# Decode attention and gated MLP on one core: a query weight shared by two key units, projections with one weight load per two banks, small inputs as long packets

## The chip, the core, the metric

One Trainium2 chip, of which the kernel uses one core of eight. The metric is the device time of one execution in microseconds (us). All times below are medians of several executions.

The engines are named as the profile does: PE is the matmul engine (PEld its weight loads), DVE the vector engine, ACT the scalar engine, SP the engine that issues the large DMAs.

## The reference, cut to what matters

One token (`S = 1`, `D = 1024`) goes through two branches, mixed by a scalar gate.

```python
g = sigmoid((x * gate_w).sum(-1))                     # gate_w [1024]
# branch A: 32 query heads, 4 key/value heads, 65536 cached keys of 128 elements
q = x @ wq                                            # wq [1024, 4096]
scores = einsum(q, repeat(k_cache)) * 128 ** -0.5     # k_cache [4, 65536, 128]
o = einsum(softmax(scores), repeat(v_cache))          # v_cache [4, 65536, 128]
a = o @ wo                                            # wo [4096, 1024]
# branch B
z = gelu(x @ w_in)                                    # w_in [1024, 3584]
z2 = layernorm(z[1792:])
b = (z[:1792] * (w_sp * z2 + b_sp)) @ w_out           # w_out [1792, 1024]; w_sp and b_sp are one value each
out = g * a + (1 - g) * b
```

Everything is bf16. The two caches are 67.1 MB each, all inputs together 162.0 MB. Each byte is used once.

## The kernel before

All engines are driven by a small recorder: `P(engine, function, r=reads, w=writes)` appends an operation. Each engine executes its operations in program order, and a semaphore wait is put in where a read or a write conflicts with an operation of another engine.

All large inputs pass through a ring of five SBUF slots of up to 4 MB, in one fixed order. A slot is loaded again as soon as its content has been used.

```python
small(vw(xT, 0, [[4, 2], [1, 4]]), A_x[0, 0].rearrange("(i p k) -> p i k", i=2, k=4), "xT")      # 8-byte pieces
small(vw(gw, 0, [[4, 2], [1, 4]]), gate_w.rearrange("(i p k) -> p i k", i=2, k=4), "gw")
small(wb[:, 0:1], bass.AP(tensor=B_w_sp.tensor, ..., ap=[[0, 128], [1, 1]]), "wsp")              # 128 x 2 bytes
small(wb[:, 1:2], bass.AP(tensor=B_b_sp.tensor, ..., ap=[[0, 128], [1, 1]]), "bsp")
# ... gate from xT and gw, then the wq matmuls; both need xT; program order puts the gate first
```

A key unit is 8192 keys. DVE transposes it in four pieces; each piece needs four matmuls whose weights are the padded query:

```python
def k_piece(n, j):                      # unit n, piece j
    P("DVE", lambda e: e.transpose(ktb(i).bitcast(F32), sl[:, 2048 * j:2048 * (j + 1)].bitcast(F32)), ...)
    def f(e):
        for fe in range(4):
            ins = e.matmul(pf(sb), qpad[g % 2][:, o:o + 128], vw(ktb(i), ...), ...)   # 128 columns, 512 wide
```

The output projection packs four matmuls into four column groups of the array, so that they run side by side (in the trace of the kernel before the first four start within 0.01 us, at 369.18 us):

```python
WO = [(0, 0, 8), (1, 0, 8), (2, 0, 8), (3, 0, 4), (3, 4, 6), (3, 6, 8)]     # chunk, first and last column
for i, c0, c1 in WO:
    for c in range(c0, c1):
        for q in range(4):
            e.matmul(pf(FB)[32 * q:32 * q + 1, 0:QW], ovec[:, 8 * i + c:...], sl[:, o:o + QW],   # QW = 256
                     tile_position=(0, 32 * q), ...)
P("DVE", lambda e: e.tensor_tensor(orow[0:97, :], pf(FB)[0:97, 0:QW], brow[0:97, :], ALU.add), ...)
```

The projection `w_out` of branch B ("wout" below) is packed in the same way into another bank, and is copied to `brow`.

## Time and profile before

| | before |
|---|---|
| time, median of its first 3 runs | 387.75 us (387.69 to 387.80) |
| span of the profiled run | 385.9 us |
| large DMA queue | 162.01 MB, 98.1% of 16 engines |
| PE, DVE busy | 59%, 55% |
| last V pair in use from | 363.2 us |

The last row is the time at which PE starts on the last load of values (one load brings a pair of value units); behind it only `wo` is still to come, in four chunks of 2 MB.

First some lines of the profile's page: the span and the busy times, the rate in 40 equal slices, the DMA queues (packets, MB, share), and two groups of instructions (busy us, mean ns of one, then the idle time before them and what ended it).

```profile
span 385.9 us, 3595 instructions
PE 227.0 (59%) x1542; PEld 84.7 (22%) x1542; DVE 210.5 (55%) x326; ACT 30.6 (8%) x71; POOL 2.1 (1%) x9
...
GB/s 326 435 435 442 374 442 426 429 436 433 435 408 419 435 435 430 428 435 427 431 431 435 433 435 431 435 423 429 435 431 426 428 432 435 430 431 428 419 419 190
...
q1 hardware_dynamic: 6200, 162.01, 98.1%
...
q10 hardware_dynamic: 832, 0.00, 0.1%
...
L457 PE MATMUL pb<-arena 128*128 128x512 bf16 x512 | 154.4, 442 | 78.5 <-DVE arena L449 76.2
L449 DVE STREAM_TRANSPOSE arena<-arena 128x1024 f32<-128x1024 f32 x128 | 151.3, 1216 | 56.7 <-DMA arena<-in_A_k_cache_dram 50.5
```

No compute engine is near full, and the DMA engines are: the stream is the limit. PE waits for DVE, and DVE for keys. At 431 GB/s the 162.0 MB take 376 us. Two slices stand out: the fifth (374) and the last.

The windows view shows this in three stretches. Its columns: start and end, length, busy time (and instructions) of PE, PEld, DVE, ACT and POOL, granted PE clock, DMA share, GB/s.

```profile
42.00:47.00 5.00, 4.87 (x48) 1.63 (x52) 0.08 (x1) 0.00 (x0) 0.00 (x0) 1.00 0.80 315
100.00:120.00 20.00, 15.95 (x115) 5.88 (x113) 19.16 (x30) 2.27 (x3) 0.00 (x0) 1.00 0.99 419
148.00:340.00 192.00, 121.80 (x684) 38.12 (x680) 121.59 (x175) 19.33 (x48) 0.00 (x0) 0.81 1.00 431
```

The steady rate is 431. The stretch of 42 to 47 us is slow at 315. I call it the hole. (The clock column of the first line says nothing: this trace has no clock record before 47.7 us, and the wq matmuls of that stretch step at 427 ns, the step of half clock.)

The chain that ended last, followed back from the end (start, length, what):

```profile
1.24 38.87 DMA arena<-in_gate_w_dram
...
42.13 6.39 PE pb L404 x64
...
146.17 1.04 PE pb L457 x4
...
369.25 1.83 PE pb L635 x28
371.08 0.02 issue
371.10 11.62 DMA arena<-in_A_wo_dram
382.72 0.04 issue
382.76 0.62 PE pb L635 x7
383.38 0.02 issue
383.41 0.42 DVE arena L641
```

A 2 KB input, `gate_w`, takes 38.9 us, and the first wq matmul (L404) comes only after it. At the end the kernel waits for the last bytes of `wo`; only 1.1 us of compute follows their landing (0.62 of packed matmuls, 0.42 of the final add).

### The profile page before, as it was taken

What the parts mean: (1) busy time and instruction counts of PE and PEld (TensorE: products, weight loads), DVE (VectorE), ACT (ScalarE), POOL (GpSimd) and SP (SyncE); (2) the same over time, 40 slices, a digit from 0 to 9 for tenths busy, and PEclk for the clock granted to TensorE, in tenths of its full rate; (3) what the DMA queues carried; (4) which work ended last, traced back from release to release, by engine and by line L of the source; (5) the groups of instructions that cost most, each with busy time, mean ns of one, the idle gap of its engine ahead of it and who ended that gap; (6) DMA issues with size and microseconds to landing.
All of it is one profiled execution on the core that took longest, in us unless ns stands there. A gap on an engine that the chain in (4) does not pass through costs nothing.

```text
span 385.9 us, 3595 instructions
## 1 busy us (share of the span) xinstructions
PE 227.0 (59%) x1542; PEld 84.7 (22%) x1542; DVE 210.5 (55%) x326; ACT 30.6 (8%) x71; POOL 2.1 (1%) x9
## 2 busy tenths in 40 slices
PE   0000668983886888472688383827883929543354
PEld 0000225562232222121222120212220202211121
DVE  4000078335999997574597574735984748511010
ACT  1000000001011110000010000000010100320000
POOL 2000000000000000000000000000000000000000
PEclk9999969695899999696789697956697978866555
DMA  8999999999999999999999999999999999999994
GB/s 326 435 435 442 374 442 426 429 436 433 435 408 419 435 435 430 428 435 427 431 431 435 433 435 431 435 423 429 435 431 426 428 432 435 430 431 428 419 419 190
DMA packets 7048, 162.24 MB, mean 420 GB/s; under 512 B 1524, under 2 KB 1528, under 8 KB 1784
## 3 DMA queue, kind: packets, MB, share of 16 engines
q1 hardware_dynamic: 6200, 162.01, 98.1%
q8 instruction: 12, 0.20, 0.2%
q10 hardware_dynamic: 832, 0.00, 0.1%
q14 instruction: 4, 0.03, 0.0%
HBM read 162.01 MB, written 0.00 MB: 420 GB/s over the span
## 4 chain that ended last, share of the span: by engine, by line
DMA 53%; PE 22%; DVE 22%; issue 1%; ACT 0%; ACTq 0%; DVEq 0%
DMA arena<-in_A_k_cache_dram 31%; DVE arena L449 16%; PE pb L457 13%; DMA arena<-in_gate_w_dram 10%; DMA arena<-in_A_v_cache_dram 9%; PE pb L543 3%; DMA arena<-in_A_wo_dram 3%; PE pb L501 2%; DVE arena L470 2%; PE pb L404 2%; DVE arena L492 1%; PE pb L635 1%; DVE arena L518 0%; DVE arena L438 0%; PE pb L523 0%
## 5 line engine op out<-in xcount | busy, mean ns | idle before, releaser
L457 PE MATMUL pb<-arena 128*128 128x512 bf16 x512 | 154.4, 442 | 78.5 <-DVE arena L449 76.2
L449 DVE STREAM_TRANSPOSE arena<-arena 128x1024 f32<-128x1024 f32 x128 | 151.3, 1216 | 56.7 <-DMA arena<-in_A_k_cache_dram 50.5
L457 PEld LDWEIGHTS pb<-arena 128*128 128x128 bf16 x512 | 45.4, 106 | 181.9 <-DVE arena L449 128.1
L501 PE MATMUL pb<-arena 128*32 128x512 bf16 x512 | 39.3, 442 | 20.3 <-DMA arena<-in_A_v_cache_dram 17.8
L487 ACT ACTIVATE arena<-arena 128x512 bf16<-128x512 f32 x32 | 23.0, 720 | 208.5 <-DVE arena L492 155.3
L492 DVE STREAM_TRANSPOSE arena<-arena 128x512 bf16<-128x512 bf16 x32 | 21.7, 679 | 18.3 <-PE pb L501 18.3
L470 DVE TENSOR_SCALAR_CACHE_REDUCE arena<-pb 128x512 f32<-128x512 f32 x32 | 21.7, 678 | 5.7 <-PE pb L457 5.5
L386 PE MATMUL pb<-arena 128*128 128x1 f32 x2 | 0.6, 364 | 40.6 <-DVE arena L385 40.6
L501 PEld LDWEIGHTS pb<-arena 128*32 128x32 bf16 x512 | 12.9, 107 | 44.5 <-issue 36.5
L384 DVE TENSOR_TENSOR arena<-arena 128x8 f32<-128x8 bf16 x1 | 0.2, 166 | 35.1 <-DMA arena<-in_gate_w_dram 35.1
L543 PEld LDWEIGHTS pb<-arena 128*128 128x128 bf16 x224 | 13.8, 161 | 0.4
L543 PE MATMUL pb<-arena 128*128 128x1 bf16 x224 | 13.7, 198 | 0.0
L635 PE MATMUL pb<-arena 128*1 128x256 bf16 x128 | 7.8, 409 | 6.3 <-DMA arena<-in_A_wo_dram 6.2
L515 DVE RECIPROCAL arena<-pb 128x1 f32<-128x1 f32 x4 | 0.7, 168 | 18.1 <-PE pb L513 18.1
L386 PEld LDWEIGHTS pb<-arena 128*128 128x128 f32 x2 | 0.5, 314 | 40.6 <-DVE arena L385 40.6
L641 DVE TENSOR_TENSOR arena<-pb,arena 97x256 bf16<-97x256 f32 x1 | 0.4, 425 | 13.4 <-PE pb L635 13.4
L404 PE MATMUL pb<-arena 128*2 128x512 bf16 x64 | 6.4, 584 | 0.9 <-DVE arena L395 0.9
L487 ACT ACTIVATION_READ_ACCUMULATOR arena<-arena 128x1 f32 x32 | 6.0, 186 | 0.0
L635 PEld LDWEIGHTS pb<-arena 128*1 128x1 bf16 x128 | 3.4, 109 | 10.5 <-DMA arena<-in_A_wo_dram 7.6
L523 PE MATMUL pb<-arena 128*128 128x128 bf16 x16 | 1.8, 243 | 5.2 <-DVE arena L518 5.2
L554 DVE COPY arena<-pb 128x28 f32<-128x28 f32 x1 | 0.2, 187 | 7.8 <-PE pb L543 7.8
L411 DVE CAST arena<-pb 98x512 bf16<-98x512 f32 x1 | 0.7, 692 | 6.5 <-PE pb L404 6.5
(81 smaller groups left out, 47.7 us busy)
## 6 DMA issues: line engine op xcount, KB each, us to landing
arena<-in_A_k_cache_dram SPq DMA_DIRECT2D x16, 4096.0 KB, 28.8
arena<-in_A_v_cache_dram SPq DMA_DIRECT2D x16, 4096.0 KB, 33.5
arena<-in_A_wq_dram SPq DMA_DIRECT2D x2, 4096.0 KB, 17.0
arena<-in_B_w_in_dram SPq DMA_DIRECT2D x2, 3584.0 KB, 27.4
arena<-in_A_wo_dram SPq DMA_DIRECT2D x3, 2048.0 KB, 34.6
arena<-in_B_w_out_dram SPq DMA_DIRECT2D x1, 3584.0 KB, 16.8
arena<-in_A_wo_dram SPq DMA_DIRECT2D x1, 1024.0 KB, 23.1
arena<-in_A_wo_dram SPq DMA_DIRECT2D x2, 512.0 KB, 13.1
```

The source lines that it names most:

```text
L386: P("PE", lambda e: e.matmul(pf(PTB)[:, 0:1], ones, col(C_GS), start=True, stop=True), r=["ones", "gs"], w=[B(PTB)])
L404: ins = e.matmul(pf(OB)[32 * cg:32 * cg + 2, :], xw[:, 3 * c + 1 - s:3 * c + 3 - s], sl[:, WQ_N * k + 512 * (4 * s + cg):WQ_N * k + 512 * ...
L411: P("DVE", lambda e: e.tensor_copy(qsb[0:98, :], pf(OB)[0:98, :]), w=[("psb", 0), B(OB)])
L449: P("DVE", lambda e: e.transpose(ktb(i).bitcast(F32), sl[:, 2048 * j:2048 * (j + 1)].bitcast(F32)), r=[key], w=[("kt", i % NKTS)])
L457: ins = e.matmul(pf(sb), qpad[g % 2][:, o:o + 128], vw(ktb(i), 64 * f2 + ev, [[128, 16], [2, 32]]), start=(j == 0 and fe == 0), stop=(j == ...
L470: P("DVE", lambda e: e.tensor_scalar(scs(n), pf(sb), 0.0, None, op0=ALU.add, op1=ALU.max, accum_out=maxc[:, n:n + 1]), w=[("sc", n % NSC), ...
L487: P("ACT", lambda e: e.activation(psb(n), scs(n), ACTF.Exp, bias=gcol(g, K_NB), scale=SCALE, accum_out=lp[:, n:n + 1]), r=[("sc", n % NSC) ...
L492: P("DVE", lambda e: e.transpose(ptsb(n), psb(n)), r=[("psb", n % 2)], w=[("ptsb", n % 2)])
L501: ins = e.matmul(pf(OB)[32 * cg:32 * (cg + 1), :], ptsb(n)[:, 32 * b:32 * (b + 1)], vw(sl, 128 * b, [[2048, 4], [1, 128]]), start=(u == 0 ...
L523: ins = e.matmul(pf(MB)[:, 0:128], sel[:, 128 * c:128 * (c + 1)], osc[:, 128 * c:128 * (c + 1)], start=(c == 0), stop=(c == 3))
L543: ins = e.matmul(pf(MB)[:, z:z + 1], vw(sl, c0, [[FC, 128]]), xT[:, 2 * i + k:2 * i + k + 1], start=(i == 0 and k == 0 and z == 0), stop=( ...
L635: ins = e.matmul(pf(FB)[32 * q:32 * q + 1, 0:QW], ovec[:, 8 * i + c:8 * i + c + 1], sl[:, o:o + QW], start=(i == 0 and c == 0), stop=(i == ...
```

## The change

Its intent is to take work off PE and to start earlier:

* the small inputs come as one or two long rows each and are spread over the partitions by PE;
* two key units use each loaded query weight: a second matmul follows without a weight load. Score banks go from two to four, transposed tiles from three to four, score buffers from ten to eight;
* both projections give up the four column groups. One weight column is used for two matmuls of 512 columns, into two banks. Only the last wo chunk stays packed.

```diff
-    small(vw(xT, ...), A_x[0, 0].rearrange("(i p k) -> p i k", i=2, k=4), "xT")
-    small(vw(gw, ...), gate_w.rearrange("(i p k) -> p i k", i=2, k=4), "gw")
-    small(wb[:, 0:1], bass.AP(tensor=B_w_sp.tensor, ..., ap=[[0, 128], [1, 1]]), "wsp")
-    small(wb[:, 1:2], bass.AP(tensor=B_b_sp.tensor, ..., ap=[[0, 128], [1, 1]]), "bsp")
+    small(xrow[0:2, :], A_x[0, 0].rearrange("(i n) -> i n", i=2), KX)
+    small(grow[0:2, :], gate_w.rearrange("(i n) -> i n", i=2), KG)
+    small(wb[0:1, 0:1], B_w_sp, "wsp")
+    small(wb[0:1, 1:2], B_b_sp.rearrange("(a n) -> a n", a=1), "bsp")
@@ (transposes of x by PE, a matmul with ones that spreads w_sp and b_sp: cut)
+    def again(e, prev, out, rhs, start, stop):          # a matmul on the weights already loaded
+        ... InstMatmult(..., ldweights=False, ins=[e.lower_ap(rhs), list(m.ins)[1]], outs=[e.lower_ap(out)])
@@ k_piece: now of a pair of units
-                ins = e.matmul(pf(sb), qpad[g % 2][:, o:o + 128], vw(ktb(i), ...), ...)
+                ins = e.matmul(pf(sb[0]), qpad[g % 2][:, o:o + 128], rhs[0], start=st, stop=sp)
+                ins = again(e, ins, pf(sb[1]), rhs[1], st, sp)
@@ both projections
+    def project(e, vec, sl, first, last):
+        for c in range(n):
+            ins = e.matmul(pf(WB0)[0:1, :], vec[:, c:c + 1], sl[:, DO * c:DO * c + 512], ...)
+            ins = again(e, ins, pf(WB1)[0:1, :], sl[:, DO * c + 512:DO * (c + 1)], st, sp)
+    def keep(first):                                     # copy to, or add into, the four rows of brow
+        for q in range(4): ... e.tensor_copy(dst, src) if first, else e.tensor_tensor(dst, src, dst, ALU.add)
@@ the end
-    for i, c0, c1 in WO:
+    for i in range(3):
+        P("PE", lambda e, ...: project(e, ovec[:, 8 * i:8 * (i + 1)], sl, i == 0, i == 2), ...)
+    keep(False)
+    FB = SCB[0]
+    P("DVE", lambda e: e.memset(pf(FB), 0.0), w=[B(FB)])
+    for i, c0, c1 in WO[3:]:                             # the last chunk: packed matmuls into FB, as before
```

More of the change, by code (lines that the diff above doesn't have):

```diff
@@ L169, in bass_gated_mix__gqa_block_cached__mixer_gmlp__decode_kernel @@
     QP = 152
-    NKTS = 3
-    NSC = 10
+    NKTS = 4
+    NSC = 8
     QW = DO // 4
@@ L189, in bass_gated_mix__gqa_block_cached__mixer_gmlp__decode_kernel @@
         ("QPAD", 2 * 4 * QP), ("IDB", 128), ("IDF", 256), ("BM", 256), ("ONES", 256), ("SEL", 16 * 32),
-        ("M16", 32), ("M8", 16), ("M32", 64), ("MQ", 32), ("OT", 256), ("XT", KC), ("GW", KC), ("WB", 2), ("MAXC", 2 * G * NU), ("LP", 2 * G * NU),
+        ("M16", 32), ("M8", 16), ("M32", 64), ("MQ", 32), ("OT", 256), ("XT", KC), ("WB", 2), ("WBB", 4), ("ONEB", 128), ("MAXC", 2 * G * NU), ("LP", 2 * G * NU),
         ("COLS", 2 * 64), ("DM", 32), ("QT", 32), ("QALL", 128), ("XW", 3 * KC), ("OSC", 512), ("OV", OC), ("Z", 2 * 28), ("Z2", 2 * 28),
@@ L211, in bass_gated_mix__gqa_block_cached__mixer_gmlp__decode_kernel @@
     m32, mq, ot = af("M32", 32), af("MQ", 16), af("OT", 128)
-    xT, gw, wb = ab("XT", KC), ab("GW", KC), ab("WB", 2)
+    xT, wb, wbb, oneb = ab("XT", KC), ab("WB", 2), af("WBB", 2), ab("ONEB", 128)
     qpad = [ab("QPAD", 4 * QP, 4 * QP * i) for i in range(2)]
@@ L238, in bass_gated_mix__gqa_block_cached__mixer_gmlp__decode_kernel @@
     FB, PTB, OB, MB = 0, 5, 6, 7
-    SCB = [3, 4]
+    WB0, WB1 = 0, 7
+    SCB = [1, 2, 3, 4]
     pf = lambda i: bank[i][:, :]
     pbf = lambda i: bank[i][:, :].bitcast(BF16)
+    def again(e, prev, out, rhs, start, stop):
+        m = prev.ins
+        return e.add_instruction(mybir.InstMatmult(
+            start_tensor_calc=start, stop_tensor_calc=stop, tile_size=m.tile_size, tile_position=m.tile_position,
+            bass_skip_group_check=True, ldweights=False, name=nc.get_next_instruction_name(), engine=e.engine,
+            ins=[e.lower_ap(rhs), list(m.ins)[1]], outs=[e.lower_ap(out)]))
     R = Recorder()
@@ L256, in bass_gated_mix__gqa_block_cached__mixer_gmlp__decode_kernel @@
     P("DVE", lambda e: e.memset(ones, 1.0), w=["ones"])
-    P("DVE", lambda e: e.memset(brow, 0.0), w=["brow"])
+    P("DVE", lambda e: e.memset(oneb, 1.0), w=["oneb"])
+    P("DVE", lambda e: e.memset(brow, 0.0), w=[("brow", q) for q in range(4)])
     P("DVE", lambda e: e.memset(pf(MB), 0.0), w=[B(MB)])
@@ L267, in f @@
                 return e.dma_start(dst, src)
-        P("ACT", f, w=[key], dma=key)
-    small(vw(xT, 0, [[4, 2], [1, 4]]), A_x[0, 0].rearrange("(i p k) -> p i k", i=2, k=4), "xT")
-    small(vw(gw, 0, [[4, 2], [1, 4]]), gate_w.rearrange("(i p k) -> p i k", i=2, k=4), "gw")
-    small(wb[:, 0:1], bass.AP(tensor=B_w_sp.tensor, offset=B_w_sp.offset, ap=[[0, 128], [1, 1]]), "wsp")
-    small(wb[:, 1:2], bass.AP(tensor=B_b_sp.tensor, offset=B_b_sp.offset, ap=[[0, 128], [1, 1]]), "bsp")
+        P("ACT", f, w=[key], dma="l%s" % (key if isinstance(key, str) else key[1]))
+    xrow, grow, prod = ab("SC", 512, (NSC - 2) * 1024), ab("SC", 512, (NSC - 3) * 1024), af("SC", 512, (NSC - 4) * 512)
+    KX, KG, KP = [("sc", NSC - i) for i in (2, 3, 4)]
+    small(xrow[0:2, :], A_x[0, 0].rearrange("(i n) -> i n", i=2), KX)
+    small(grow[0:2, :], gate_w.rearrange("(i n) -> i n", i=2), KG)
+    small(wb[0:1, 0:1], B_w_sp, "wsp")
+    small(wb[0:1, 1:2], B_b_sp.rearrange("(a n) -> a n", a=1), "bsp")
     stream = []
@@ L381, in bass_gated_mix__gqa_block_cached__mixer_gmlp__decode_kernel, with f @@
           r=["idb"], w=[KSE])
-    P("DVE", lambda e: e.tensor_tensor(z2[:, 0:KC], xT, gw, ALU.mult), r=["xT", "gw"], w=["z2"])
-    P("DVE", lambda e: e.tensor_reduce(col(C_GS), z2[:, 0:KC], AXX, ALU.add), r=["z2"], w=["gs"])
-    P("PE", lambda e: e.matmul(pf(PTB)[:, 0:1], ones, col(C_GS), start=True, stop=True),
+    def f(e):
+        for c in range(4):
+            ins = e.transpose(pbf(PTB)[:, 2 * c:2 * c + 2], vw(xrow, c, [[4, 128]], 0, 2), idb[0:2, 0:2])
+        return ins
+    P("PE", f, r=[KX, "idb"], w=[B(PTB)])
+    P("DVE", lambda e: e.tensor_copy(vw(xT, 0, [[4, 2], [1, 4]]), vw(pbf(PTB), 0, [[1, 2], [2, 4]])),
+      w=["xT", B(PTB)])
+    P("DVE", lambda e: e.tensor_copy(vw(xw, 1, [[3, KC]]), xT), r=["xT"], w=["xw"])
+    P("PE", lambda e: e.matmul(pf(MB)[:, 0:2], oneb[0:1, :], wb[0:1, :], start=True, stop=True),
+      r=["oneb", "wsp", "bsp"], w=[B(MB)])
+    P("DVE", lambda e: e.tensor_copy(wbb, pf(MB)[:, 0:2]), w=["wbb", B(MB)])
+    P("DVE", lambda e: e.tensor_tensor(prod[0:2, :], xrow[0:2, :], grow[0:2, :], ALU.mult), r=[KX, KG], w=[KP])
+    P("DVE", lambda e: e.tensor_reduce(col(C_GS)[0:2, :], prod[0:2, :], AXX, ALU.add), r=[KP], w=["gs"])
+    P("PE", lambda e: e.matmul(pf(PTB)[:, 0:1], ones[0:2, :], col(C_GS)[0:2, :], start=True, stop=True),
       r=["ones", "gs"], w=[B(PTB)])
@@ L392, in bass_gated_mix__gqa_block_cached__mixer_gmlp__decode_kernel @@
       r=["g"], w=["omg"])
-    P("DVE", lambda e: e.tensor_copy(vw(xw, 1, [[3, KC]]), xT), r=["xT"], w=["xw"])
     for i in range(4):
@@ L445, in k_piece @@
             q_piece(g)
-        sl, key = use(("k", n))
         i = nbatch[0]
-        nbatch[0] += 1
-        P("DVE", lambda e: e.transpose(ktb(i).bitcast(F32), sl[:, 2048 * j:2048 * (j + 1)].bitcast(F32)),
-          r=[key], w=[("kt", i % NKTS)])
-        sb = SCB[n % 2]
+        nbatch[0] += 2
+        sb = [SCB[n % 4], SCB[n % 4 + 1]]
+        for m in range(2):
+            sl, key = use(("k", n + m))
+            P("DVE", lambda e, m=m, sl=sl: e.transpose(ktb(i + m).bitcast(F32),
+                                                       sl[:, 2048 * j:2048 * (j + 1)].bitcast(F32)),
+              r=[key], w=[("kt", (i + m) % NKTS)])
         def f(e):
@@ L456, in f @@
                 o = QP * fe + 24 - 8 * j
-                ins = e.matmul(pf(sb), qpad[g % 2][:, o:o + 128], vw(ktb(i), 64 * f2 + ev, [[128, 16], [2, 32]]),
-                               start=(j == 0 and fe == 0), stop=(j == 3 and fe == 3))
-            return ins
-        P("PE", f, r=[("qpad", g % 2), ("kt", i % NKTS)], w=[B(sb)])
-        if pend:
+                rhs = [vw(ktb(i + m), 64 * f2 + ev, [[128, 16], [2, 32]]) for m in range(2)]
+                st, sp = j == 0 and fe == 0, j == 3 and fe == 3
+                ins = e.matmul(pf(sb[0]), qpad[g % 2][:, o:o + 128], rhs[0], start=st, stop=sp)
+                ins = again(e, ins, pf(sb[1]), rhs[1], st, sp)
+            return ins
+        P("PE", f, r=[("qpad", g % 2), ("kt", i % NKTS), ("kt", (i + 1) % NKTS)], w=[B(sb[0]), B(sb[1])])
+        while pend:
             score_piece(pend.pop(0))
         if j == 3:
-            done(("k", n))
-            pend.append(n)
+            done(("k", n + 1))
+            pend.extend([n, n + 1])
     def score_piece(n):
         g, u = KV[n]
-        sb = SCB[n % 2]
+        sb = SCB[n % 4]
         P("DVE", lambda e: e.tensor_scalar(scs(n), pf(sb), 0.0, None, op0=ALU.add, op1=ALU.max,
@@ L576, in mixer_piece @@
         P("DVE", lambda e: e.reciprocal(col(C_R1), col(C_S1)), r=["s1"], w=["r1"])
-        P("DVE", lambda e: e.scalar_tensor_tensor(col(C_AL), col(C_R1), 2.0, wb[:, 0:1], op0=ALU.mult, op1=ALU.mult),
-          r=["r1", "wsp"], w=["al"])
-        P("DVE", lambda e: e.tensor_copy(col(C_BE), wb[:, 1:2]), r=["bsp"], w=["be"])
+        P("DVE", lambda e: e.scalar_tensor_tensor(col(C_AL), col(C_R1), 2.0, wbb[:, 0:1], op0=ALU.mult, op1=ALU.mult),
+          r=["r1", "wbb"], w=["al"])
+        P("DVE", lambda e: e.tensor_copy(col(C_BE), wbb[:, 1:2]), r=["wbb"], w=["be"])
         P("DVE", lambda e: e.tensor_scalar(z2[:, 0:FC], ze[:, 0:FC], col(C_AL), col(C_BE), op0=ALU.mult, op1=ALU.add),
@@ L583, in mixer_piece @@
           r=["z2", "omg", "zg"], w=["yb"])
+    def project(e, vec, sl, first, last):
+        n = vec.shape[1]
+        for c in range(n):
+            st, sp = first and c == 0, last and c == n - 1
+            ins = e.matmul(pf(WB0)[0:1, :], vec[:, c:c + 1], sl[:, DO * c:DO * c + 512], start=st, stop=sp,
+                           skip_group_check=True)
+            ins = again(e, ins, pf(WB1)[0:1, :], sl[:, DO * c + 512:DO * (c + 1)], st, sp)
+        return ins
     def wout_piece(i):
         sl, key = use(("wout", i))
-        def f(e):
-            for c in range(7):
-                for q in range(4):
-                    ins = e.matmul(pf(MB)[32 * q:32 * q + 1, 0:QW], yb[:, 7 * i + c:7 * i + c + 1],
-                                   sl[:, DO * c + QW * q:DO * c + QW * (q + 1)],
-                                   start=(i == 0 and c == 0), stop=(i == 1 and c == 6), tile_position=(0, 32 * q),
-                                   skip_group_check=True)
-            return ins
-        P("PE", f, r=["yb", key], w=[B(MB)])
+        P("PE", lambda e: project(e, yb[:, 7 * i:7 * (i + 1)], sl, i == 0, i == 1), r=["yb", key], w=[B(WB0), B(WB1)])
         done(("wout", i))
         if i == 1:
-            P("ACT", lambda e: e.activation(brow[0:97, :], pf(MB)[0:97, 0:QW], ACTF.Copy), w=["brow", B(MB)])
+            keep(True)
+    def keep(first):
+        for q in range(4):
+            src = pf((WB0, WB1)[q // 2])[0:1, QW * (q % 2):QW * (q % 2 + 1)]
+            dst = brow[32 * q:32 * q + 1, :]
+            k = [B((WB0, WB1)[q // 2])]
+            if first:
+                P("DVE", lambda e, dst=dst, src=src: e.tensor_copy(dst, src), w=[("brow", q)] + k)
+            else:
+                P("DVE", lambda e, dst=dst, src=src: e.tensor_tensor(dst, src, dst, ALU.add), r=[("brow", q)],
+                  w=[("brow", q)] + k)
     started = set()
@@ L610, in bass_gated_mix__gqa_block_cached__mixer_gmlp__decode_kernel @@
         nxt = steps[si + 1][1] if si + 1 < len(steps) else None
-        if k is None and pend:
+        while k is None and pend:
             score_piece(pend.pop(0))
@@ L615, in bass_gated_mix__gqa_block_cached__mixer_gmlp__decode_kernel @@
         for j in range(4):
-            if k is not None:
-                k_piece(k, j)
+            if k is not None and j % 2 == 0:
+                k_piece(k - k % 2, 2 * (k % 2) + j // 2)
             if j == 1 and v is not None:
@@ L625, in bass_gated_mix__gqa_block_cached__mixer_gmlp__decode_kernel @@
             (win_piece if a[0] == "win" else wout_piece)(a[1])
-    for i, c0, c1 in WO:
+    for i in range(3):
+        sl, key = use(("wo", i, 0))
+        P("PE", lambda e, i=i, sl=sl: project(e, ovec[:, 8 * i:8 * (i + 1)], sl, i == 0, i == 2), r=[("ovec", i), key],
+          w=[B(WB0), B(WB1)])
+        done(("wo", i, 0))
+    keep(False)
+    FB = SCB[0]
+    P("DVE", lambda e: e.memset(pf(FB), 0.0), w=[B(FB)])
+    for i, c0, c1 in WO[3:]:
         sl, key = use(("wo", i, c0))
@@ L635, in f @@
                     ins = e.matmul(pf(FB)[32 * q:32 * q + 1, 0:QW], ovec[:, 8 * i + c:8 * i + c + 1],
-                                   sl[:, o:o + QW], start=(i == 0 and c == 0), stop=(i == 3 and c == 7),
+                                   sl[:, o:o + QW], start=(c == 0), stop=(c == 7),
                                    tile_position=(0, 32 * q), skip_group_check=True)
@@ L641, in bass_gated_mix__gqa_block_cached__mixer_gmlp__decode_kernel @@
     P("DVE", lambda e: e.tensor_tensor(orow[0:97, :], pf(FB)[0:97, 0:QW], brow[0:97, :], ALU.add),
-      r=["brow"], w=["orow", B(FB)])
+      r=[("brow", q) for q in range(4)], w=["orow", B(FB)])
     osrc = bass.AP(tensor=arena, offset=OFF["OROW"], ap=[[32 * NA, 4], [1, QW]])
```

## The prediction

> **What bounds it now.** The stream of caches and weights. The page's DMA part shows 162.0 MB at 98.1% of 16 engines; windows of 40 to 60 us between 148 and 340 us run at 430 to 432 GB/s whatever the compute engines do (PE busy 59%, DVE 55%). At 431 GB/s the stream takes 376 of the 385.9 us. The Trainium skill ("DMA: Bandwidth & Descriptors", Specifications) gives a ceiling of 435 GB/s; the trace agrees (431): the rate has no room.
>
> Holes, from windows: 42 to 47 us at 315 GB/s (1.3 us lost), 100 to 120 us at 419 (about 0.6 us). Both follow from the late start: the chain begins with the gate_w load, which lands 38.9 us after issue; PE first touches wq at 42.1, the first ring slot is refilled at 45.8, when the 20.4 MB loaded at the start have nearly run dry, and compute drags behind until 148.
>
> **What the change removes.** (a) The late start. The four small inputs (landing 22, 39, 49 and 57 us after issue; 832 packets) become a few long packets that should land within 10 us; wq starts as it lands (about 12 us), slot 0 is refilled near 20 us, the holes close: 1.8 us, on the critical path. (b) Half of the 512 query weight loads. Warm, 4 matmuls take 1.05 us (262 ns each) where 512 columns alone should need 215; cold they step at 427 ns, the load hidden. At most 15 to 20 us of PE time, off the path: PE and DVE wait for the caches there. (c) Score buffers 10 to 8: exp runs before its slot is needed; no cost.
>
> **What it adds.** The wo projection loses its four-column-group packing. Before, a 2 MB chunk is 32 matmuls of 256 columns, four at a time: 1.88 us at half clock. After, 16 matmuls of 512 columns in sequence: 6.8 us cold, 3.5 us warm. Before, PE waited for data here (chunks at 369.2, 372.9, 377.8); after, PE is the limit. The Trainium skill ("TensorE: Matmul & The Clock Gate", Part 1) says the clock doubles after about 3.4 us of sustained work; the trace agrees (3.0 to 5.5 us in eight bursts; even the wq matmuls with 2 weight columns quickened near 47.6). In before's times: chunk 0 from 369.5 to 375, chunk 1 to 378.7, chunk 2 to 382.2; then four DVE adds (0.4 us each, from the final add's 425 ns) and a PSUM memset (485 ns) before the last chunk's matmuls: 384.3; these 1 us (warm), final add: 385.7 against 383.8. The tail loses about 2 us and gives back what (a) gains. If one-column matmuls do not raise the clock, it loses about 10 us.
>
> **Prediction.** 387.9 us, range 385.5 to 395. Faster by over 2%: 0.03; within 2%: 0.83; slower: 0.14.
>
> **What would show it.** Right: small loads within 10 us, first wq matmul before 15 us; 42 to 47 us at about 430 GB/s; last cache load lands about 1.8 us earlier; query weight loads halved, PE busy down; at the chain's end waits for wo data are replaced by PE on the projection, then DVE adds and memset.
>
> **What would make it wrong.** The clock staying at half through the projection (+9 us, slower). Small packets costing the stream more than seen, so that the last landing moves by more than 2 us (faster, down to 384). Pairing turning PE or DVE into a limit in the cache stages.

## More of the kernel before

With the clock up, four key matmuls take 1.04 us from the first start to the modelled end of the last; they start 216 to 230 ns apart (146.17, 146.40, 146.62 and 146.84).

## The result, and the profile after

| | before | after |
|---|---|---|
| time, median of 6 runs | 387.72 us (387.49 to 388.95) | 388.60 us (387.95 to 389.19) |
| ratio after to before | | 1.0019, 95% interval 1.0002 to 1.0036 |
| span of the profiled run | 385.9 us | 386.2 us |
| packets of the small inputs | 832 | 12 |
| last V pair in use from | 363.2 us | 362.0 us |

Ratios here and below are the mean time of one kernel's runs over the mean of the other's of the same rounds, so they are not quite the ratios of the quoted medians. By the 2% measure the two kernels are the same; after is 0.2% slower.

The page of after. PE line numbers have moved: L486 is the first matmul of a key pair, L247 the second of a pair, in the keys and in the projections alike.

```profile
span 386.2 us, 3169 instructions
PE 237.5 (62%) x1471; PEld 66.8 (17%) x1177; DVE 214.6 (56%) x338; ACT 30.0 (8%) x70; POOL 2.1 (1%) x9
...
GB/s 330 434 434 438 426 432 433 433 434 434 434 434 431 433 424 428 431 423 434 431 431 428 433 431 434 429 434 432 434 434 433 431 425 431 436 417 428 421 419 105
...
q10 hardware_dynamic: 12, 0.00, 0.0%
...
L476 DVE STREAM_TRANSPOSE arena<-arena 128x1024 f32<-128x1024 f32 x128 | 149.1, 1212 | 67.2 <-DMA arena<-in_A_k_cache_dram 60.9
L486 PE MATMUL pb<-arena 128*128 128x512 bf16 x256 | 116.9, 456 | 95.5 <-DVE arena L476 88.8
```

The fifth slice went from 374 to 426 GB/s. The windows:

```profile
42.00:47.00 5.00, 4.27 (x38) 2.07 (x31) 1.74 (x2) 0.00 (x0) 0.00 (x0) 1.00 0.98 419
100.00:120.00 20.00, 12.95 (x45) 2.51 (x22) 15.56 (x26) 1.52 (x4) 0.00 (x0) 0.81 0.98 423
148.00:340.00 192.00, 117.80 (x673) 27.41 (x524) 118.07 (x174) 18.30 (x46) 0.00 (x0) 0.79 1.00 431
```

The hole is gone, the stretch of 100 to 120 us is hardly better, and the steady rate is the same although the weight loads in it fell from 680 to 524. The last V pair comes into use 1.24 us earlier (361.98 against 363.22).

The end is another one. From the timeline (start, busy us, engine, line, operation, and the idle time before it with what ended it):

```profile
13.03 0.16 PE L405 MATMUL pb<-arena 1*128 1x2 bf16 x1 [10.10 <-DMA arena<-in_B_b_sp_dram]
...
15.25 3.58 PE L428 MATMUL pb<-arena 128*2 128x512 bf16 x32
...
376.58 0.38 PE L619 MATMUL pb<-arena 128*1 128x512 bf16 x1
...
379.81 0.38 PE L247 MATMUL pb<-arena 128*1 128x512 bf16 x1
380.23 1.70 DVE L640 TENSOR_TENSOR arena<-pb,arena 1x256 f32<-1x256 f32 x4 [12.14 <-PE pb L247]
382.03 0.48 DVE L677 MEMSET pb<- 128x512 f32 x1
382.57 0.75 PEld L685 LDWEIGHTS pb<-arena 128*1 128x1 bf16 x32 [3.11 <-DVE pb L677]
382.57 1.04 PE L685 MATMUL pb<-arena 128*1 128x256 bf16 x32 [2.38 <-DVE pb L677]
383.67 0.42 DVE L691 TENSOR_TENSOR arena<-pb,arena 97x256 bf16<-97x256 f32 x1 [1.15 <-PE pb L685]
```

The third wo chunk lands at 376.5, and its 16 matmuls keep PE busy to 380.2. The four adds follow (1.70), the memset (0.48), then the packed matmuls of the last chunk (1.04), which PE has been waiting to start for 2.38 us, and the final add. The last bytes had landed by 381 us: the windows of one us after it show no stream. What was gained at the start was thus given back behind the stream.

### The profile page after: what moved, and what is told of

It is laid out like the page before. It is cut to its first block, busy times and chain, and to the rows that moved or that the text cites. A ratio compares the mean times of both kernels' runs of the same rounds, so it can differ in the third digit from the quotient of the medians.

```text
span 386.2 us, 3169 instructions
## 1 busy us (share of the span) xinstructions
PE 237.5 (62%) x1471; PEld 66.8 (17%) x1177; DVE 214.6 (56%) x338; ACT 30.0 (8%) x70; POOL 2.1 (1%) x9
## 4 chain that ended last, share of the span: by engine, by line
DMA 62%; PE 19%; DVE 17%; issue 1%; SPq 0%; DVEq 0%
DMA arena<-in_A_k_cache_dram 53%; DVE arena L476 13%; DMA arena<-in_A_v_cache_dram 10%; PE pb L247 7%; PE pb L486 5%; PE pb L619 2%; PE pb L530 2%; PE pb L572 2%; DVE arena L499 2%; DVE arena L521 1%; DVE arena L640 0%; DVE arena L638 0%; DVE arena L547 0%; PE pb L685 0%; PE pb L552 0%
## 5 line engine op out<-in xcount | busy, mean ns | idle before, releaser
L476 DVE STREAM_TRANSPOSE arena<-arena 128x1024 f32<-128x1024 f32 x128 | 149.1, 1212 | 67.2 <-DMA arena<-in_A_k_cache_dram 60.9
L486 PE MATMUL pb<-arena 128*128 128x512 bf16 x256 | 116.9, 456 | 95.5 <-DVE arena L476 88.8
L247 PE MATMUL pb<-arena 128*128 128x512 bf16 (+1 forms) x294 | 131.5, 447 | 0.0
L486 PEld LDWEIGHTS pb<-arena 128*128 128x128 bf16 x256 | 27.9, 109 | 208.1 <-DVE arena L476 123.0
L499 DVE TENSOR_SCALAR_CACHE_REDUCE arena<-pb 128x512 f32<-128x512 f32 x32 | 20.4, 672 | 2.5 <-PE pb L247 2.5
L530 PEld LDWEIGHTS pb<-arena 128*32 128x32 bf16 x512 | 13.0, 108 | 49.7 <-issue 41.8
L619 PE MATMUL pb<-arena 128*1 128x512 bf16 x38 | 15.4, 406 | 0.5 <-DVE arena L556 0.5
L572 PEld LDWEIGHTS pb<-arena 128*128 128x128 bf16 x224 | 13.8, 159 | 0.8 <-issue 0.7
L428 PE MATMUL pb<-arena 128*2 128x512 bf16 x64 | 7.2, 627 | 3.9 <-DMA arena<-in_A_wq_dram 3.9
L640 DVE TENSOR_TENSOR arena<-pb,arena 1x256 f32<-1x256 f32 x4 | 1.7, 415 | 12.2 <-PE pb L247 12.1
L638 DVE COPY arena<-pb 1x256 f32<-1x256 f32 x4 | 1.7, 414 | 8.2 <-PE pb L247 8.1
(91 smaller groups left out, 49.7 us busy)
```

What stands on the lines that cost most here:

```text
L247: return e.add_instruction(mybir.InstMatmult(start_tensor_calc=start, stop_tensor_calc=stop, tile_size=m.tile_size, tile_position=m.tile_p ...
L428: ins = e.matmul(pf(OB)[32 * cg:32 * cg + 2, :], xw[:, 3 * c + 1 - s:3 * c + 3 - s], sl[:, WQ_N * k + 512 * (4 * s + cg):WQ_N * k + 512 * ...
L476: P("DVE", lambda e, m=m, sl=sl: e.transpose(ktb(i + m).bitcast(F32), sl[:, 2048 * j:2048 * (j + 1)].bitcast(F32)), r=[key], w=[("kt", (i ...
L486: ins = e.matmul(pf(sb[0]), qpad[g % 2][:, o:o + 128], rhs[0], start=st, stop=sp)
L499: P("DVE", lambda e: e.tensor_scalar(scs(n), pf(sb), 0.0, None, op0=ALU.add, op1=ALU.max, accum_out=maxc[:, n:n + 1]), w=[("sc", n % NSC), ...
L530: ins = e.matmul(pf(OB)[32 * cg:32 * (cg + 1), :], ptsb(n)[:, 32 * b:32 * (b + 1)], vw(sl, 128 * b, [[2048, 4], [1, 128]]), start=(u == 0 ...
```

## The experiments

Twelve kernels were run, in three groups, each group on its own chip; the kernel before had a median of 387.70, 387.77 and 387.68 us beside them. All gave correct results. The ratios are to the kernel before.

| kernel | median us (range) | ratio (95%) | last V pair from, us |
|---|---|---|---|
| small inputs only | 386.57 (386.34 to 386.87) | 0.9971 (0.9959 to 0.9983) | 362.3 |
| pairing only | 387.84 (387.61 to 387.90) | 1.0002 (0.9990 to 1.0014) | 363.0 |
| projections only | 391.78 (389.49 to 395.18) | 1.0109 (1.0073 to 1.0145) | 363.4 |
| small inputs and pairing | 386.68 (386.55 to 386.70) | 0.9971 (0.9958 to 0.9984) | 362.1 |
| wo projection only | 389.28 (389.06 to 391.47) | 1.0041 (1.0028 to 1.0054) | 363.3 |
| wout projection only | 389.30 (388.34 to 391.21) | 1.0041 (1.0023 to 1.0060) | 364.3 |
| small inputs and projections | 388.44 (388.15 to 389.05) | 1.0018 (1.0006 to 1.0030) | 362.0 |
| after, third chunk packed | 386.26 (386.19 to 386.41) | 0.9962 (0.9950 to 0.9974) | 361.9 |
| small inputs, late start kept | 386.55 (386.50 to 387.13) | 0.9970 (0.9958 to 0.9982) | 362.0 |
| after, memset early | 386.61 (386.39 to 387.74) | 0.9967 (0.9954 to 0.9979) | 362.1 |
| after, clock kept up | 388.55 (387.99 to 389.25) | 1.0019 (1.0007 to 1.0031) | 362.3 |
| combined | 386.67 (386.44 to 387.62) | 0.9975 (0.9963 to 0.9987) | 362.0 |

### Group 1: the three parts of the change, each alone

The edits are the hunks of the diff above: the first (small inputs), the `k_piece` hunk with its buffers (pairing), and `project`, `keep` and the end (projections).

> The kernel before with the small inputs' part alone. My theory (the earlier start closes the stream's hole near 42 us, all later landings move up, the tail is untouched): 386.2 us, 385.7 to 386.7, ratio about 0.996; first wq matmul near 15 us; 42 to 47 us at 415 GB/s or more; the last V pair's matmuls start 1.0 to 1.8 us earlier than before's 363.2. Rival A (the stream's end is fixed by its rate, a hole early is made up later): 387.7, ratio 1.000, last V at 363.

> The kernel before with the pairing of key units and the buffer sizes alone. My theory (off the critical path): 387.7 us, within 0.3 us of the kernel before, with 256 instead of 512 query weight loads. Rival B (pairing delays the caches' ring slots or the scores and costs in the cache stages): 388.5 us or more, last V later than 363.2. Rival C (pairing speeds the caches' stages up): 387 or less.

> The kernel before with the two projections' part alone. My theory (the end now waits for the third wo chunk's 16 sequential matmuls, four adds and a memset): 389.7 us, 389.2 to 390.7, ratio about 1.005, last V still at 363.2; in the end of the chain 3.5 us of projection matmuls, 1.7 us of adds, 0.5 us of memset. Rival A (the end is fixed by the wo bytes): 387.7 us.

> The kernel after with the projections put back to the four column groups of before. My theory: as the small inputs alone, 386.2 us (385.7 to 386.7), 2.0 to 2.5 us less than after's 388.6, faster than both kernels. Rival B (pairing costs what the small inputs give): 387.7 us or more.

**Measured.** The small inputs give 1.1 us (0.29%), the pairing nothing, both together the same 1.0. The pairing lowered the PE busy time from 227.0 to 221.9 us, and none of it reached the end. Rival A of the small inputs and rivals B and C of the pairing fall. The projections alone cost 4.1 us where I had expected 2.0, and single runs were spread over 5.7 us. That was a miss, and it asked for the next group. (The profiled run was its fastest, 389.49 us, so no trace shows one of the long ones.) In the full change the projections cost only 388.60 - 386.68 = 1.9 us.

### Group 2: which projection, and what absorbs it

The edits: the projections' part with the old packed `wout_piece` (wo only) or with the old packed end (wout only); the full change without the pairing; and the full change with the third chunk packed (the start and stop flags that move with it are cut):

```diff
-    for i in range(3):
+    for i in range(2):
-    for i, c0, c1 in WO[3:]:
+    for i, c0, c1 in WO[2:]:
```

> The kernel before with only the wo projection (the end) changed, the wout projection packed as before. The projections' part alone measured 391.8 us with single runs from 389.5 to 395.2, where I had expected 389.7. Theory 1 (the end costs what I expected, and the rest and the spread come from the wout projection in the stage near 110 us, where the ring of this late starting kernel has nearly run dry): 389.7 us, spread under 1.5 us, last V pair as in the kernel before. Theory 2 (the spread is the PE clock coming up at different moments in the end): median near 391.5, single runs from 389.5 to 395.

> The kernel before with only the wout projection changed, the end as before. Theory 1: 389 to 390 us, with single runs several us apart, the last V pair later than before's 363.2. Theory 2: 387.7 us, no spread.

> The kernel after without the pairing (small inputs and projections). Theory 1 (the early start gives the ring enough reserve to absorb the wout projection): 388.6 us as after, spread about 1.5 us. Rival: it is the pairing (four transposed tiles instead of three, four score banks) that absorbs it, and this one runs at 390 us or more with the spread of the projections' part alone.

> The kernel after with the third wo chunk packed in four column groups like the last one, so that only two chunks go one matmul after another and the adds and the memset run while the third chunk still loads. My theory (what costs in the end of after is the sequence behind the landing of the third chunk: 3.5 us of matmuls, 1.7 of adds, 0.5 of memset): 386.7 us, as the kernel with the old projections. Rival (the two first chunks' sequential matmuls are the limit already): 387.7 or more.

**Measured.** The wo projection at the end costs 1.5 us (expected: 2.0, with a spread under 1.5, which was 2.4), and the wout projection, which I had not counted at all, costs the same. The wout matmuls now occupy PE for 6.1 us instead of 1.7, DVE stands still meanwhile, and the ring is refilled late: the V load that the kernel before issued at 128.6 us comes at 136.2. The timeline and the windows of the wout kernel, then the same windows of the kernel before:

```profile
115.65 1.70 DVE L618 COPY arena<-pb 1x256 f32<-1x256 f32 x4 [7.28 <-PE pb L247]
...
116.00:120.00 4.00, 1.04 (x4) 0.31 (x4) 3.95 (x8) 0.00 (x0) 0.00 (x0) 1.00 0.96 352
...
136.00:140.00 4.00, 3.92 (x29) 1.24 (x28) 4.00 (x7) 0.23 (x1) 0.00 (x0) 1.00 0.83 295
...
116.00:120.00 4.00, 2.16 (x10) 0.70 (x8) 3.38 (x10) 0.60 (x1) 0.00 (x0) 1.00 0.99 418
...
136.00:140.00 4.00, 3.33 (x24) 0.93 (x16) 4.00 (x6) 0.81 (x2) 0.00 (x0) 1.00 1.01 434
```

The kernel before has 418 and 434 GB/s in these two stretches, the one with small inputs and projections 401 and 451. The reserve can be summed from the traces, as bytes of the loads issued less bytes of the packets that have ended: between 112 and 145 us the wout kernel falls to 0.65 MB, at 135.9 us, and the one with small inputs and projections never below 5.9 MB. So the wout kernel has no reserve for the stall, and its last V pair comes 1.0 us later (364.3). With the small inputs' part the stall costs nothing that shows: small inputs and projections together run at 388.4 us like after, and the pairing is not needed for it. ("After, third chunk packed" below keeps the unpacked wout projection and, at 386.26 us, is not slower than "combined", 386.67, which packs it.) Theory 1 holds in its main point. That the early start makes the reserve, and not the long packets, is read from traces only: between 96 and 112 us "small inputs only" never holds less than 8.6 MB, "small inputs, late start kept" of group 3 falls to 2.2 and the kernel before to 1.2. No run put the unpacked wout projection into the late starting kernel with long packets.

Theory 2 has a share too. In the profiled run of the wo kernel, which was its slowest (391.47 us), the clock came up late and was lost again. Its windows:

```profile
370.00:375.00 5.00, 5.00 (x13) 0.77 (x6) 0.04 (x1) 0.00 (x0) 0.00 (x0) 0.50 0.99 423
376.00:382.00 6.00, 6.00 (x29) 1.18 (x14) 0.00 (x0) 0.00 (x0) 0.00 (x0) 1.00 0.72 294
385.00:387.20 2.20, 1.88 (x32) 0.97 (x32) 0.22 (x2) 0.00 (x0) 0.00 (x0) 0.57 0.00 0
```

The projection ran at half clock (0.50) for 5.3 us from its start at 369.8, where after's ran so for 3.4, and the last packed matmuls took 1.88 us where after's took 1.04. By my estimate (half of 1.9, and 0.84) that makes about 1.8 us against after's end, in one run. It does not explain the spread of the projections' part: of its six runs the longest (395.18 us) has the highest mean clock, 0.834, and the shortest (389.49) 0.826. Together the two costs account for 3.0 of the 4.1 us of the projections' part; the rest lies within its spread, and I did not trace it further.

With the third chunk packed the whole loss at the end goes away: 386.26 us, the fastest kernel, 0.38% faster than before and faster than after. The rival (the first two chunks are the limit already) falls. Its end waits for the last bytes again:

```profile
378.77 1.91 PE L685 MATMUL pb<-arena 128*1 128x256 bf16 x56 [2.47 <-DVE pb L677]
381.52 0.39 PE L685 MATMUL pb<-arena 128*1 128x256 bf16 x8 [0.85 <-DMA arena<-in_A_wo_dram]
```

### Group 3: the cause of the hole, and the end once more

The edits, in this order: the wq matmuls of "small inputs only" wait for the first w_in load too; the memset moved up; 14 idle matmuls before the last V pair; and a combination.

```diff
-        P("PE", f, r=["xw", key], w=[B(OB)])
+        P("PE", f, r=["xw", key, ("slot", 3)], w=[B(OB)])
```
```diff
+    FB = SCB[0]
+    P("DVE", lambda e: e.memset(pf(FB), 0.0), w=[B(FB)])
     for i in range(3):
         ... project ...
     keep(False)
-    FB = SCB[0]
-    P("DVE", lambda e: e.memset(pf(FB), 0.0), w=[B(FB)])
```
```diff
+                if v == total - 2:
+                    warm_piece()      # 14 x e.matmul(pf(SCB[1]), qpad[1][:, 0:128], ktb(0)[:, 0:512], ...)
                 pv_piece(v)
```

> The small inputs' part alone, but the first wq matmul made to wait for the first w_in load as well (it lands near 41 us), so that the long packets stay and only the early start is taken away. My theory (the gain comes from the early start, which refills the ring in time): 387.7 us again, the hole from 42 to 47 us back at about 320 GB/s, last V near 363.2. Rival (the fewer packets themselves speed the stream up): 386.6 us.

> The kernel after with the memset of the last chunk's bank moved ahead of the projection, so that it runs while PE is busy. My theory (the memset lies on the path at the end): 0.5 us less than after, 388.1 us. Rival: no change, 388.6.

> The kernel after with 14 matmuls without a use (128 columns, 512 wide, into a free score bank) in the 6 us in which PE waits for the last V pair, so that the clock is up when the projection begins. If the moment at which the clock comes up sets the difference between after's single runs (387.95 to 389.19): the end waits for the third chunk's landing in every run, about 388.0 us with a spread under 0.4 us. If the clock does not matter there: 388.6 with the same spread.

> The kernel with the third chunk packed (386.3 us), the wout projection packed as before as well, the memset early and the last half megabyte of wo loaded in two pieces. Expected 386.0 us, 385.7 to 386.4: the end is set by the landing of the last bytes, little is left to win there.

**The late start.** My theory falls. With the start put back to 41.2 us (before: 42.1) the gain stays whole, 386.55 us, and there is no hole:

```profile
42.00:47.00 5.00, 4.19 (x63) 1.51 (x56) 0.69 (x1) 0.00 (x0) 0.00 (x0) 1.00 0.97 419
```

Its ring is refilled at 44.4 and 46.1 us, the one of before at 45.8 and 48.5, so the two differ by 1.4 to 2.4 us there and are not quite equal. But the reserve, summed as above, sinks as low in both: to 2.36 MB before and 2.62 MB here. The DMA packet records of the traces tell more. In both kernels the fifth load of the ring, of keys, is under way in this stretch, as groups of 16 packets of 32 KB, one per DMA engine. The time from the start of one group to the next, and the small packets counted in it:

```
                   time to the next group, us                    small packets per group
before:            1.22 1.26 1.44 1.45 1.39 1.32 1.22 1.23       16 to 31, nearly all of 2 bytes (w_sp)
late start kept:   1.21 1.21 1.21 1.21 1.21 1.21 1.21 1.22       none
                   mean time of one packet of the group, us
before:            1.22 1.23 1.30 1.32 1.38 1.28 1.27 1.21
late start kept:   1.21 to 1.22 in all
```

The load was under way throughout, so the engines of the kernel before had not run dry of requests. Its groups took 10.53 - 9.69 = 0.84 us longer in all. Of this about 0.5 us is that the packets themselves took longer; the rest is pauses between packets, the longest of 0.14 and 0.13 us in the third and fourth group. Before this load the kernel with long packets was already 0.3 us ahead (17 MB landed at 42.6 against 42.9 us), about what the 512 packets of 8 bytes took of each DMA engine's time, 0.29 us. The three kernels that kept the small inputs' old form and whose records I looked at (pairing only, projections only, wout only) show the same, with groups of up to 1.5 us. In the one whose wq matmuls ended early, at 47.2, the slow groups went on to 49.7 us, so the wq matmuls alone do not explain them. The hole therefore belongs to the old form of the small inputs, not to the late start: that the new form cures it is shown. What exactly makes it is not. The 8-byte packets had ended by 38.6 us. It falls together with the 2-byte packets of `w_sp`, but the first groups beside these (1.22 us) are hardly slower, and the like packets of `b_sp` that follow alternate with packets of 28 KB that keep their 1.06 us. Kernels that change only the 2-byte or only the 8-byte inputs would tell these apart.

**The memset.** Moving one memset gives 2.0 us (ratio 0.9967 against after's 1.0019), four times what I had expected, and makes the full change faster than the kernel before. I had counted only the memset's own 0.48 us. From the timeline:

```profile
381.31 0.38 PE L247 MATMUL pb<-arena 128*1 128x512 bf16 x1
381.31 0.95 PEld L685 LDWEIGHTS pb<-arena 128*1 128x1 bf16 x26 [0.34 <-issue]
381.32 1.25 PE L685 MATMUL pb<-arena 128*1 128x256 bf16 x26
381.73 1.70 DVE L640 TENSOR_TENSOR arena<-pb,arena 1x256 f32<-1x256 f32 x4 [12.30 <-PE pb L247]
383.46 0.42 DVE L691 TENSOR_TENSOR arena<-pb,arena 97x256 bf16<-97x256 f32 x1
```

The packed matmuls of the last chunk need nothing from the four adds. But they need the cleared bank, and DVE does its work in program order, so the memset behind the adds made PE wait for the adds as well. With the memset early the packed matmuls (L685) follow the projection at once and run beside the adds: the adds' 1.70 us alone are left of 1.70 + 0.48 + 1.04. Those other two terms are 1.5 us, and the small waits between them another 0.2; the remaining 0.3 of the 2.0 us is not traced (in after, from the last projection matmul's start at 379.81 to the final add at 383.67 it is 3.86 us, here from 381.31 to 383.46 it is 2.15). This profiled run was this kernel's slowest (387.74 us); its clock came up only at 373.9 us.

**The clock.** Keeping PE busy before the last V pair changed nothing: 388.55 us with the same spread. The windows of this run:

```profile
363.00:367.00 4.00, 1.94 (x30) 0.97 (x22) 1.81 (x5) 0.00 (x0) 0.00 (x0) 1.00 0.98 418
368.00:370.00 2.00, 2.00 (x6) 0.38 (x3) 0.00 (x0) 0.00 (x0) 0.00 (x0) 0.50 0.98 418
371.00:376.00 5.00, 4.88 (x23) 0.84 (x10) 0.00 (x0) 0.00 (x0) 0.00 (x0) 1.00 0.99 415
```

The clock was up in the V matmuls and fell back in the pauses behind them, so the experiment did not do what it was made for. It still says something: PE then waited 1.05 us for the third chunk, which it did not do for more than 0.4 us in after, and the time was no better. By this one run, the end of after hangs on the landing of the third chunk and what follows, not on how quickly the first two are done. Where the spread of after's single runs (1.2 us) comes from stays open.

**The combination** was no better than its parts: 386.67 us against 386.26 for the third chunk packed. The expected 0.3 us from smaller last pieces did not come, and I did not look further.

## Why the prediction was right

The time (388.60 against 387.9, range 385.5 to 395) and the class were right, and so was the main sum: something over 1 us gained at the stream's start, about 2 us lost at its end. That the number came so close has luck in it. The gain was over-estimated (1.8 against 1.1) and put down to the wrong cause, and the wout projection, not counted at all, happened to cost nothing in the full change. Point by point:

* **The stream is the limit: right.** The steady rate is 431 to 432 GB/s in every kernel, near the 435 of the Trainium skill ("DMA: Bandwidth & Descriptors", Specifications), and the pairing alone moved the time by 0.02%.
* **"(a) The late start ... slot 0 is refilled near 20 us, the holes close: 1.8 us": the size was off and the cause named was wrong.** The gain is 1.1 us. The first hole closed, 315 to 419 GB/s; the second hardly did, 419 to 423. And the gain does not come from the start: with the late start kept it was as large. Beside the old packets the stream was slower. The prediction had small packets that cost the stream only in its list of what would make it wrong. The first refill of slot 0 did come early, at 18.9 us.
* **The early start has another worth that I did not name:** it gives the ring a reserve. Without the small inputs' part the wout projection costs 1.5 us, with it nothing that shows; that this goes by the start is read from the reserve in the traces and not shown by a run.
* **"Small loads within 10 us, first wq matmul before 15 us": nearly.** The last of them (`b_sp`) was waited for until 13.0 us, and the first wq matmul started at 15.25.
* **The pairing: right, off the path, but "262 ns each" was a misreading.** It divides by four a time that runs to the modelled end of the last matmul. From start to start the key matmuls of the kernel before, with a weight load for each, step at 219 ns (median with the clock up), those of after at 217. The loads were thus hidden with the clock up too, and the "15 to 20 us of PE time" were not there: PE was busy 5.1 us less. "PE busy down" was wrong for the whole change: it rose from 227.0 to 237.5 us. The unpacked projections put more on than the pairing took off (projections alone: 236.4).
* **"The wo projection loses its four-column-group packing ... the tail loses about 2 us": right, 1.9 us** (388.60 against 386.68), with the predicted parts: adds 1.70 (predicted 1.6), memset 0.48, last matmuls 1.04. The step "chunk 1 to 378.7, chunk 2 to 382.2" in before's times was a little off: after's PE was done with chunk 1 at 376.4 and waited for the third chunk's data until 376.58, so the landing and not PE decided when it began.
* **The clock rises with one-column weights: right.** In after it was at 1.00 from 371.8 us, 4.0 us after the projection began and after 3.4 us at half clock, close to what the Trainium skill has ("TensorE: Matmul & The Clock Gate", Part 1: about 3.4 us of sustained work). In one run of the wo kernel it took 5.3 us.
* **What I missed in the sum:** that the memset, by its place in DVE's order, put the last matmuls behind the adds. I had written these terms one after the other and had not asked whether they had to be so. Moved up, this one line turns the change from 0.2% slower into 0.3% faster than before.

## What to carry to other kernels

In a kernel bound by its stream, count a change by what it does before the first and around the last bytes; 5 us less PE busy time in the middle gave nothing here, while 2 us of serial work at the end cost 2 us. Read the end of such a kernel operation by operation, and ask of each wait whether the data or only an engine's program order demands it: a memset that could have run long before held the last matmuls behind four adds. Read the step of an instruction from start to start, not from the length of a merged row. And when a slow stretch falls together with a late start, test them apart before naming the one the cause of the other.

## What the Trainium skill lacked or had wrong

* "TensorE: Matmul & The Clock Gate", Back-to-back issue gap, gives a sustained 131 ns per matmul of 512 columns in streams of weight load and matmul. No run here comes near: with the clock up the steps were 219 ns (median) with a 128-column weight load for each matmul, 217 ns with one load for two, 216 ns in the projection. The last agrees with the 215.7 ns of the same page's Part 1.
* The same page, Part 2, lets the next weights load while this matmul runs. The trace agrees, at half clock (427 ns a step, loads included) and with the clock up, where a load for each matmul added some 2 ns to the step (219 against 217).
* The same page, Part 1, does not say whether weights of a single column count as activity for the clock: they do (0.50 to 1.00 after 4.0 and 5.3 us of the projection). It names an idle window of about 3.4 us for the fall, and further on tells of falls through frequent short pauses without a size; here the clock fell to 0.50 although PE was busy for 1.94 of the 4 us before and no pause was longer than 1.4 us.
* The same page, Part 3, has no figure for four column groups with 1-column weights: at half clock, 32 matmuls of 256 columns took 1.88 us packed, where 16 of 512 one after another would take 16 x 427 ns = 6.8 us.
* "DMA: Bandwidth & Descriptors", Queues, rings and completion order, tells of the round robin between queues packet by packet; the trace agrees (16 small packets for 16 large ones, so that the 2 KB of `gate_w`, behind the 2 KB of `x`, took 38.9 us). No page has a figure for what small packets cost the large ones of another queue: here the step of 32 KB packets went from 1.21 to up to 1.45 us in a stretch with 2-byte packets, and the old form of four inputs of 4 KB in all cost 1.1 us. Which part of it does so is open.
